# One transfer of X made four, and another order of the front, in an adaLN, H3 and SwiGLU kernel

## The chip, the cores and the metric

The kernel runs on one core of a Trainium2 chip. The metric is the device time of one execution in microseconds; the median of three runs before the change is 581.48 us (580.92 to 582.07).

## The reference, cut to what matters

One sequence of S = 2048 positions and D = 512 channels passes an adaLN layer with two branches. The first is the H3 operator: a causal convolution of 4 taps on K, a product with V, a causal convolution as long as the sequence, and a gate. The second is a SwiGLU feed-forward net with F = 1792.

```python
kv = shift_conv(k, shift_k) * v                  # 4 taps per channel
kv_f = rfft2(pad(kv)); kf_f = rfft2(pad(ssm_k))  # over 2 S points
y = irfft2(kv_f * kf_f)[:S] + kv * ssm_D
A = q * y                                        # q is layernorm(x)*(1+ca)+sa
...
mod = silu(c) @ w_mod                            # sa, ca, ga, sb, cb, gb
x = x + ga * A
h = layernorm(x) * (1 + cb) + sb
x = x + gb * ((silu(h @ w_gate) * (h @ w_up)) @ w_down)
```

Inputs and output are float32.

## The kernel before, in words

**Two parts.** The front (up to `next_psum()`) computes the H3 branch, the modulation rows, the second norm and the first two blocks of the feed-forward net. The main part is a loop over 28 steps (`gate_up_first`, `gate_up`) that does the rest of the feed-forward net with seven products of blocks for each eight; its first matmuls write the tiles named `a` and `b`.

**The front by chunks.** The 512 channels are four chunks `c_` of 128. For each chunk:

- `tap0`, `tap`, or `tms` with `tma`, make the short convolution, and `times_v` the product with V, in four pieces. Chunk 0 has its own way, by matmuls with diagonal tiles for one half (`diag`, `x0_taps`, `x0_mul`; tile `kvt`), and by VectorE for the other (`p_tap0`, `p_tap`, `p_mul`, turned by `p_turn`).
- `x_turn` brings the product to the layout of positions, `x_first` does the first stage of the transform (tile `s1`, in the profile `s`), `k_first` and `k_turn` the same for the kernel `ssm_k` (tiles `s` and `kt`). `skip` adds `ssm_D` to the first row of `ssm_k`.
- `swap_x(n)` transposes blocks of 32 by 32 of `X` in place on VectorE, a quarter of a chunk at a time.
- The second stage goes by half chunks `n`: `x3(n, m)` (tile `px`), `x_sum`, then `product3(n, m)` for m = 0, 1, 2 (a matmul into `pk`, and on VectorE the product with `xs`), and `inv3(n)`, 48 matmuls into `iv`, of which two copies on ScalarE write back to `X`.
- Chunk 0, 1 and 2 then need an exchange between partitions: `put(c_)` writes `X[c_]`, 128 partitions of 16 KB, to memory (`away`), and `get(c_)` reads it back in four transfers, one for each 32 partitions, transposed. Chunk 3 does it by VectorE (`inv3s`).
- `y_pe(t, chunks)` is the last stage of the transform (tile `y`), for the quarter `t` of the positions. `y_into` multiplies by the gate `s` and adds to `x`; `y_gate` and `add_y` do it in two steps.

The gate `s` is made from `x` by `do_stats` or `a_sum` and `a_var`, by `gate_n` (two rows of 512 each) and by `gate_p` (two operations with `bcs`). The modulation rows need `w_mod` in three parts of two halves, 1024 KB each (`mod_load(p, h)`, tile `wm`); parts 0 and 1 go over `mod_mul`, `mod_part` and `mod_bc`, part 2 over `mod_row(2, h)` (tile `mr`), `mod_out` and `mod_T`. Then `rs1` to `rs3`, `norm1`, `norm_t` (tile `nt`), `norm_s` and the splits into two parts (`hi1`, `lo1`) make the operands of the net, and `gu_pe` its first two blocks (tile `g`). `w8_hi` and `w8_lo` split the weights of those.

`warm(n)` is n matmuls of the identity with itself; nothing reads what they give.

**What sets the order.** Each engine does its instructions in the order of the program (`InOrder`). The front is one list of some 390 calls (from line 1204), in an order that is written out, and many calls name the engine (`e=act`, `e=dve`, `e=pool`). SyncE (SP) issues all DMAs of the front in the list's order; a `put` that waits for its data holds up the DMAs behind it. Which buffer a tile gets is written out too: `SLOTS` (line 53) has a string of digits for each pool, one digit for each allocation in the order of the list. The pool `ps` has four pairs of PSUM banks, so a matmul into a new tile waits until the tile that had this pair before has been read.

Of the kernel before, what the change touches and what calls it, by code (L numbers as in the profile page):

```python
# [43 lines left out]
def adaln_h3_swiglu(ctx, tc, q, k0, v0, kT, vT, ssm, dskip, wgu, wdn, wmod, e_fwd, e_inv, w_c, out):  # L44
# [9 lines left out]
        "e8": "301245670142561074612740340143104134104134104134150364051304650314056304",  # L54
        "b16": "0112345024024453024",
        "k2": "012021021020121020121020121020121020121020121012021012021012021012021012021012021012",
        "ps": "012301230123012031203120312031203120312013201320132013210321032103103210321032103210321032102310231023102310321032103210321213120023012120310",
        "r4": "01234012430012342013424301430123403402143201342014320134201432013420143240310234213014324031",
        "one": "456723017425036241736412506425173421750621507341573062570634170346250362417364125064251730256731546317027513643105725601341076526370140753623157047561321065745630120376546713025",
# [1143 lines left out]

    load_k0(0)
    diag(0, e=act)
    diag(2, e=dve)
    load_k0(1)
    warm(16)
    small_in(e=act)
    p_tap0(e=dve)  # L1210
    p_tap(1, 0, e=dve)
    p_tap(2, 0, e=dve)
    load_v0(0)
    load_k(1)
    silu_c()
    load_dskip()
    p_tap(1, 1, e=dve)
    p_tap(2, 1, e=dve)
    p_tap(3, 0, e=dve)
    diag(1, e=act)  # L1220
    diag(3, e=act)
    x0_taps(0)
    load_v0(1)
    x0_mul(0)
    tap0(1, e=act)
    load_e(0)
    load_e(1)
    p_tap(3, 1, e=dve)
    p_mul(1, e=pool)
    x0_taps(1)  # L1230
    p_mul(0, e=dve)
    p_turn(e=act)
    load_e(3)
    load_ssm(0, 0)
    load_e(2)
    x0_mul(1)
    x_first(0, 0, e=act)
# [12 lines left out]
    load_v(2)  # L1250
    swap_x(2)
    swap_x(3)
    k_first(0, 2, e=act)
    k_first(0, 1, e=act)
    times_v(1, 2, e=pool)
    k_first(0, 3, e=act)
    times_v(1, 1, e=pool)
    k_first(0, 0, e=act)
    tap0(2, e=act)
    warm(5)  # L1260
    k_turn(0, 0, e=act)
    k_turn(0, 1, e=dve)
    tap(2, 1)
    times_v(1, 0, e=pool)
    k_turn(0, 2, e=act)
    x_turn(1, 1, e=act)
    k_turn(0, 3, e=act)
    tap(2, 2)
    load_ssm(1)
    x_turn(1, 0, e=act)  # L1270
    k_first(1, 3, e=act)
    skip(1, e=pool)
    k_first(1, 0, e=act)
    x_first(1, 0, e=act)
    k_first(1, 1, e=act)
    k_first(1, 2, e=act)
    mod_rep(e=dve)
    x_first(1, 1, e=act)
    load_wc()
    load_k(3)  # L1280
    k_turn(1, 0, e=act)
    k_turn(1, 3, e=act)
    tap(2, 3)
    times_v(2, 0, e=pool)
    times_v(2, 1, e=pool)
    tap0(3, e=dve)
    x_turn(2, 0, e=act)
    times_v(2, 3, e=pool)
    x3(1, 1, e=act)
    swap_x(1)  # L1290
    load_x(1)
    x3(1, 2, e=act)
    swap_x(0)
# [23 lines left out]
    mod_mul(0, 0, e=act)
    load_ssm(2)
    product3(1, 2)
    product3(0, 1)  # L1320
    product3(0, 2)
    product3(1, 0)
    k_turn(1, 2, e=act)
    x_first(2, 1, e=act)
    swap_x(7)
    swap_x(5)
    load_v(3)
    mod_load(1)
    swap_x(8)
    mod_part(0, 0, e=pool)  # L1330
    load_x(0)
    tma(3, 3, 2, e=pool)
    load_einv()
    times_v(3, 1, e=pool)
    skip(2, e=dve)
    mod_mul(0, 1, e=act)
    times_v(3, 2, e=pool)
    inv3(1, e=act)
    inv3(0, e=act)
    put(0)  # L1340
    load_x(2)
    load_x(3)
    times_v(3, 3, e=pool)
    k_turn(1, 1, e=act)
    swap_x(10)
    x3(3, 2, e=dve)
    x3(2, 1, e=act)
    x3(3, 1, e=act)
    swap_x(9)
    skip(3, e=dve)  # L1350
    times_v(3, 0, e=pool)
    k_first(2, 0, e=act)
    k_first(2, 2, e=act)
    x_sum(3, e=dve)
    get(0)
    x3(2, 2, e=act)
    x_sum(2, e=pool)
    mod_mul(1, 0, e=act)
    mod_part(1, 0, e=pool)
    product3(3, 2)  # L1360
    product3(3, 0)
    product3(3, 1)
    mod_mul(1, 1, e=act)
    product3(2, 0)
    product3(2, 2)
    mod_part(1, 1, e=pool)
    mod_part(0, 1, e=pool)
    mod_part(0, 2, e=pool)
    do_stats(1, 0)
    mod_part(1, 2, e=pool)  # L1370
    product3(2, 1)
    k_first(2, 3, e=act)
    k_first(2, 1, e=act)
    x_turn(3, 0, e=act)
    inv3(3, e=act)
    inv3(2, e=act)
    do_stats(2, 0)
    k_turn(2, 0, e=act)
    x_turn(3, 1, e=act)
    k_turn(2, 1, e=act)  # L1380
    k_turn(2, 3, e=act)
    swap_x(11)
    put(1)
    get(1)
    x_first(3, 0, e=act)
    mod_part(0, 3, e=pool)
    mod_part(1, 3, e=pool)
    mod_bc(1)
    do_stats(0, 0)
    do_stats(0, 1)  # L1390
    do_stats(1, 1)
    x_first(3, 1, e=act)
    do_stats(2, 1)
    mod_bc(0)
    x3(5, 1, e=act)
    x3(5, 2, e=act)
    x3(4, 2, e=act)
    k_turn(2, 2, e=act)
    do_stats(3, 0)
    do_stats(3, 1)  # L1400
    x3(4, 1, e=act)
    x_sum(4, e=pool)
    swap_x(14)
    x_sum(5, e=pool)
    mod_mix()
    gate_n(2, 0, e=dve)
    k_first(3, 1, e=act)
    k_first(3, 0, e=act)
    k_first(3, 2, e=act)
    gate_n(0, 0, e=act)  # L1410
    gate_p(0, 0, 1, e=pool)
    load_w(1)
    k_first(3, 3, e=act)
    gate_n(3, 0, e=act)
    swap_x(15)
    swap_x(12)
    gate_n(0, 1, e=act)
    gate_p(0, 2, 1, e=pool)
    gate_n(1, 0, e=act)
    product3(4, 0)  # L1420
    product3(4, 2)
    gate_n(2, 1, e=act)
    product3(5, 0)
    product3(4, 1)
    product3(5, 1)
    product3(5, 2)
    swap_x(13)
# [18 lines left out]
    gate_p(3, 0, 1, e=dve)
    gate_p(3, 2, 1, e=pool)
    k_turn(3, 3, e=act)
    gate_p(0, 1, 1, e=dve)
    x3(6, 1, e=act)  # L1450
    y_into(0, 0, 1)
    x3(6, 2, e=act)
# [48 lines left out]
    y_gate(2, 2, 3)
    warm(5)
    norm_t(0, 1)
    norm_s(0, 1, e=act)
    acts_room()
    wd_hi(0)
    y_into(1, 0, 1)
    y_into(1, 2, 3)
    rs1(1)
# [4 lines left out]
    lo1("B11", 1, e=dve)
    norm_s(0, 3, e=act)
    lo1("B11", 0, e=pool)
    hi1("B21", 0, e=act)
    gate_p(3, 3, 1, e=pool)
    y_gate(3, 0, 1)
    add_y(3, 0, 4, (0, 1), e=dve)  # L1520
    rs2(1)
    rs3(1)
    y_pe(3, 2, 3)
    lo1("B21", 0, e=pool)
    y_gate(3, 2, 3)
    norm1(1, 0, e=act)
    norm1(1, 1, e=act)
    gu_pe(0, 0, 0)
    hi1("B21", 1, e=act)
    lo1("B21", 1, e=dve)  # L1530
    add_y(3, 0, 4, (2, 3), e=dve)
    norm1(1, 2, e=act)
    room()
# [245 lines left out]
```

## Time and profile before

| | before |
|---|---|
| median of the runs | 581.48 us |
| the profiled execution | 579.46 us |
| its span on the core | 577.7 us |
| granted TensorE clock | 1.00 |
| PE busy | 571.7 us (99%) |
| PE weight loads busy | 462.5 us (80%) |
| DVE busy | 448.3 us (78%) |
| ACT busy | 306.4 us (53%) |
| POOL busy | 318.0 us (55%) |

The difference between the profiled execution's time and its span, 1.8 us, lies around the span. PE is TensorE, PEld its weight loads, DVE is VectorE, ACT is ScalarE, POOL is GpSimd, SP is SyncE, whose queue (SPq) issues the DMAs. All operations are recorded at line 40, the helper that keeps the order, so the tiles' names tell them apart: `y<-X,ei` is the operation that reads `X` and `ei` and writes `y`.

A row of a timeline has start and length in us, the engine, the operation with its tiles, the number of records in it, and in brackets the recorded idle time before it and what ended it. Rows of PE carry the modelled end of the last matmul, so a row is a little longer than the distance to the next one. A row of the stretches has the window, its length and, for PE, PEld, DVE, ACT and POOL, the busy us with the number of instructions, then the granted clock, the DMA engines' share and GB/s. A row of groups has busy us and mean ns of one.

### The profile page before, as it was taken

The numbers are of one execution on the slowest core, as the hardware profiler recorded it, in microseconds if no ns is written. First come the engines' busy times: TensorE is split into PE (matmuls) and PEld (weight loads), VectorE is DVE, ScalarE is ACT, GpSimd is POOL, SyncE is SP. The second block draws the span as 40 slices with busy tenths as digits, with TensorE's granted clock in tenths as the row PEclk, the third lists the DMA queues.
The fourth block names the chain that finished last, engine by engine and source line by source line (L and its number), as shares of the span: only waits on it lengthen the run. The fifth ranks groups of instructions, "written<-read, shape, count | busy, mean of one in ns | idle before, by whom it ended". The sixth has DMA issues, their size and how long they took to land.

```text
span 577.7 us, 10729 instructions
## 1 busy us (share of the span) xinstructions
PE 571.7 (99%) x4262; PEld 462.5 (80%) x4262; DVE 448.3 (78%) x622; ACT 306.4 (53%) x471; POOL 318.0 (55%) x298
## 2 busy tenths in 40 slices
PE   9999999999999999999999999999999999999997
PEld 9985476546888888888887888888888888888886
DVE  4999999998998766666576579858686868686766
ACT  3999989951754544445454566343424343434330
POOL 1349897689737866757475676461606161515210
PEclk9999999999999999999999999999999999999999
DMA  8966998998215454284939970454343434343403
GB/s 315 411 256 261 379 251 227 235 235 205 69 37 200 148 216 165 40 281 145 283 140 257 250 319 1 149 190 171 117 160 124 160 123 161 127 162 127 163 1 145
DMA packets 54435, 106.98 MB, mean 185 GB/s; under 512 B 19441, under 2 KB 36209, under 8 KB 48370
## 3 DMA queue, kind: packets, MB, share of 16 engines
q1 hardware_dynamic: 54386, 106.31, 56.0%
q8 instruction: 33, 0.54, 0.4%
q14 instruction: 16, 0.13, 0.1%
HBM read 71.69 MB, written 34.60 MB: 184 GB/s over the span
## 4 chain that ended last, share of the span: by engine, by line
PE 86%; DVE 5%; DMA 4%; ACT 1%; SPq 1%; issue 1%; POOL 0%; ACTq 0%; POOLq 0%; DVEq 0%
PE a L40 22%; PE dn L40 14%; PE c L40 11%; PE b L40 6%; PE da L40 6%; PE s L40 4%; PE g L40 4%; PE dc L40 3%; PE iv L40 3%; PE pk L40 3%; DMA wm<-in_wmod 2%; PE kvt L40 2%; PE px L40 2%; DMA away<-X 1%; PE kt L40 1%; PE db L40 1%
## 5 line engine op out<-in xcount | busy, mean ns | idle before, releaser
L40 PE MATMUL a<-op,wsum 128*128 128x512 f32 x432 | 110.9, 392 | 0.3 <-ACT r L40 0.2
L40 PEld LDWEIGHTS a<-op,wsum 128*128 128x128 f32 x432 | 78.7, 188 | 15.7 <-ACT r L40 0.7
L40 PE MATMUL dn<-wd,acts 128*128 128x512 f32 x360 | 90.4, 389 | 0.0
L40 PEld LDWEIGHTS dn<-wd,acts 128*128 128x128 f32 x360 | 67.5, 188 | 14.0
L40 ACT COPY p<-a 128x512 f32<-128x512 f32 x50 | 29.3, 587 | 57.2 <-PE a L40 57.2
L40 POOL TENSOR_TENSOR wa<-ws,wa 128x512 fp32r<-128x512 f32 (+1 forms) x28 | 32.9, 1196 | 41.1 <-ACT wa L40 41.1
L40 DVE TENSOR_TENSOR x<-x,dn 128x512 f32<-128x512 f32 (+1 forms) x65 | 43.4, 672 | 12.8 <-PE dn L40 12.5
L40 POOL TENSOR_TENSOR tb<-wds 128x256 f32<-128x256 f32 x12 | 8.9, 740 | 64.1 <-DVE wds L40 64.1
L40 DVE TENSOR_TENSOR b<-r,c 128x512 f32<-128x512 f32 x24 | 16.7, 696 | 32.9 <-ACT sg L40 32.9
L40 ACT COPY r<-a 128x512 f32<-128x512 f32 x24 | 14.1, 586 | 50.7 <-PE a L40 50.7
L40 PE MATMUL c<-op,wa 128*128 128x512 f32 x156 | 40.0, 392 | 0.0
L40 PE MATMUL c<-op,wsum 128*128 128x512 f32 x156 | 39.6, 389 | 0.0
L40 DVE STREAM_TRANSPOSE X<-X 128x1024 f32<-128x1024 f32 x16 | 37.6, 2415 | 0.8 <-ACT X L40 0.8
L40 POOL TENSOR_TENSOR wsum<-sr,wsum 128x512 fp32r<-128x512 f32 x28 | 38.1, 1381 | 0.0
L40 PE MATMUL b<-op,wa 128*128 128x512 f32 x144 | 36.9, 391 | 0.0
L40 POOL TENSOR_TENSOR wd<-wds,wd 128x512 fp32r<-128x512 f32 x14 | 18.3, 1329 | 29.1 <-ACT wd L40 29.1
L40 PEld LDWEIGHTS c<-op,wsum 128*128 128x128 f32 x156 | 29.3, 188 | 6.1
L40 DVE TENSOR_TENSOR x<-x,da 128x512 f32<-128x512 f32 x48 | 32.7, 681 | 1.2 <-PE da L40 1.1
L40 PEld LDWEIGHTS c<-op,wa 128*128 128x128 f32 x156 | 28.5, 188 | 5.7 <-DVE b L40 0.4
L40 PEld LDWEIGHTS b<-op,wa 128*128 128x128 f32 x144 | 26.3, 188 | 4.9
L40 POOL TENSOR_TENSOR s<-s,bcs 128x512 f32<-128x512 f32 x22 | 28.0, 1287 | 0.9
L40 POOL TENSOR_TENSOR sr<-ws 128x256 f32<-128x256 f32 x28 | 24.8, 885 | 5.3 <-issue 4.4
(193 smaller groups left out, 1351.1 us busy)
## 6 DMA issues: line engine op xcount, KB each, us to landing
ds<-wsum SPq DMA_DIRECT2D x12, 1024.0 KB, 8.0
wsum<-ds SPq DMA_DIRECT2D x12, 1024.0 KB, 6.4
dw<-wa SPq DMA_DIRECT2D x12, 768.0 KB, 6.3
wa<-dw SPq DMA_DIRECT2D x12, 768.0 KB, 4.3
ws<-in_wgu SPq DMA_DIRECT2D x16, 512.0 KB, 5.4
wds<-in_wdn SPq DMA_DIRECT2D x14, 512.0 KB, 7.1
wm<-in_wmod SPq DMA_DIRECT2D x6, 1024.0 KB, 10.1
away<-X SPq DMA_DIRECT2D x3, 2048.0 KB, 11.8
```

What stands on the lines that cost most here:

```text
L40: return lambda *a, **k: self.tc.keep_in_program_order(f(*a, **k))
```

## The change: four transfers for one, and a new list

`put` is changed, all digit strings of `SLOTS` are new, and the list of the front is in another order, with another engine named in 35 of the calls; the diff is cut to the first lines of each. The calls are the same set, `warm` with 26 matmuls in all among them.

```diff
     def put(c_, name="away"):
         away[c_] = dp.tile([P, 32, P], F32, tag=f"{name}{c_}", name=f"{name}{c_}")
-        sp.dma_start(away[c_], X[c_])
+        for q_ in range(4):
+            sp.dma_start(away[c_][32 * q_ : 32 * q_ + 32], X[c_][32 * q_ : 32 * q_ + 32])
...
-        "b16": "0112345024024453024",
...
+        "b16": "0123450232053310453",
...
+    warm(5)
     load_k0(0)
+    load_k0(1)
     diag(0, e=act)
-    diag(2, e=dve)
-    load_k0(1)
     warm(16)
```

The `warm` calls stood at three places: 16 behind the first loads, 5 ahead of `k_turn(0, 0)`, 5 ahead of `norm_t(0, 1)`. Now 5 stand at the very start, 16 behind the first loads as before, and 5 ahead of `inv3(4)`. `x0_mul(1)` stood ahead of `tap(1, 1)` and now stands behind it. `w8_lo(1)` went from POOL to DVE and from behind `y_pe(0, 2)` to the place ahead of `y_into(0, 0, 1)`. Between `y_pe(0, 2)` and the first `norm_t` stood three calls of `y_pe`, and now stand four: `y_pe(3, 2, 3)`, `y_pe(2, 2, 3)`, `y_pe(1, 0, 1)`, `y_pe(1, 2, 3)`.

The calls that name another engine, by the engine they had and the one they have now:

| from, to | calls |
|---|---|
| ACT to DVE | diag(3), small_in, tap0(2), tms(3, 2), k_turn(1, 0), norm1(1, 1), hi1 of B21, second half |
| POOL to DVE | p_mul(1), x_sum(1), times_v(2, 0), tma(3, 2, 1), tma(3, 2, 2), mod_part(1, 1), gate_p(0, 2), gate_p(0, 3), gate_p(3, 2), w8_lo(1), lo1 of B21, first half |
| DVE to ACT | diag(2), k_turn(0, 1), mod_rep, tap0(3), x3(3, 2), gate_n(2, 0), norm_s(1, 3) |
| DVE to POOL | skip(0), skip(2), skip(3), times_v(2, 2), x_sum(3), gate_p(2, 2), gate_p(1, 0), gate_p(3, 0), lo1 of B11, second half, add_y(2, 0, 4, (0, 1)) |

Three places show what moved. The first is SP's queue around `put(2)`; `away_1498` and `X_558` before are chunk 2 with its copy in memory, `wm` is the third part of `w_mod`, `ws` and `wds` are weights of the net. Before:

```order
L40 DMA ws<-in_wgu 128x1024
L40 DMA away_1498<-X_558 128x4096
L40 DMA wm<-in_wmod 128x2048
L40 DMA X_558<-away_1498 32x32x128 x4
L40 DMA wm<-in_wmod 128x2048
L40 DMA ws<-in_wgu 128x1024 x2
L40 DMA wds<-in_wdn 128x2x512
```

After, with chunk 2 named `X_775` and `away_1511`, and the table of the last stage, `ei`, ahead of it:

```order
L40 DMA ei<-in_e_inv 128x2048
L40 DMA ws<-in_wgu 128x1024
L40 DMA away_1511<-X_775 32x4096 x4
L40 DMA wm<-in_wmod 128x2048 x2
L40 DMA X_775<-away_1511 32x32x128 x4
L40 DMA wds<-in_wdn 128x2x512
L40 DMA ws<-in_wgu 128x1024 x2
```

Four transfers of 32 partitions stand for one of 128, and both halves of `wm` are ahead of the four reads of `get(2)`, where one was.

The second place is the opening of DVE: `u` with `k` are the `p_tap` calls of chunk 0, `x` is `x0_mul`, `v` is `p_mul`, and `u` with `kt` and `sm` is `tap(1, t)`. Before:

```order
L40 TENSOR_SCALAR dg<-ident,k_96 128x128
L40 TENSOR_SCALAR u_120<-k_96 128x1024
L40 SCALAR_TENSOR_TENSOR u_120<-k_96,u_120 128x512 x5
L40 TENSOR_TENSOR x_153<-kvt,v_124 128x512
L40 SCALAR_TENSOR_TENSOR u_120<-k_96,u_120 128x512
L40 TENSOR_TENSOR v_124<-u_120,v_124 128x512
L40 TENSOR_TENSOR x_153<-kvt,v_124 128x512
L40 SCALAR_TENSOR_TENSOR u_155<-kt_126,sm,u_155 128x2047
```

After:

```order
L40 TENSOR_SCALAR u_124<-k_102 128x1024
L40 TENSOR_SCALAR dg<-ident,k_102 128x128
L40 COPY sm<-k_102 128x24
L40 SCALAR_TENSOR_TENSOR u_124<-k_102,u_124 128x512 x6
L40 TENSOR_TENSOR x_163<-kvt,v_126 128x512
L40 TENSOR_TENSOR v_126<-u_124,v_126 128x512 x2
L40 SCALAR_TENSOR_TENSOR u_168<-kt_132,sm,u_168 128x2047
L40 TENSOR_TENSOR x_163<-kvt,v_126 128x512
```

All six `p_tap` now stand ahead of the first product, both `p_mul` are on DVE, and the first tap of chunk 1 stands ahead of the second product with `kvt`.

The third place is ACT ahead of the copies that write chunk 2 back to `X` behind `inv3(4)` and `inv3(5)`. `s` with `x` and `rsa` are rows of `gate_n`, `kt` copies are those of `k_first(3, ...)`, and `bcs` with `pb` is `mod_bc(1)`. Before:

```order
L40 ACTIVATE s_1327<-x_718,rsa_1156 128x512 x2
L40 COPY kt_1293<-s_1334 128x4x4x32 x2
L40 ACTIVATE s_1290<-x_790,rsa_1265 128x512 x2
L40 ACTIVATE s_1327<-x_718,rsa_1156 128x512 x2
L40 ACTIVATE s_1353<-x_518,rsa_1167 128x512 x2
L40 ACTIVATE s_1290<-x_788,rsa_1198 128x512 x2
L40 COPY X_558<-iv 128x32x32 x4
```

After:

```order
L40 COPY kt_1285<-s_1321 128x4x4x32 x2
L40 COPY bcs<-pb_1343 128x2x512
L40 ACTIVATE s_1347<-x_877,rsa_1173 128x512 x2
L40 ACTIVATE s_1374<-x_773,rsa_1275 128x512 x2
L40 ACTIVATE s_1403<-x_729,rsa_1142 128x512 x2
L40 ACTIVATE s_1403<-x_888,rsa_1131 128x512 x4
L40 ACTIVATE s_1374<-x_773,rsa_1275 128x512 x2
L40 COPY X_775<-iv 128x32x32 x4
```

Twelve rows of `gate_n` and the copy of `mod_bc(1)` stand in a row between the last `kt` copies and the copies to `X`, where eight rows stood behind the last `kt` copies.

More of the change, by code (lines that the diff above doesn't have):

```diff
@@ L1219, in adaln_h3_swiglu @@
-    p_tap(3, 0, e=dve)
-    diag(1, e=act)
[L1221 to L1225, printed above, removed]
+    p_tap(3, 1, e=dve)
+    diag(2, e=act)
+    load_v0(1)
+    diag(1, e=act)
     load_e(0)
     load_e(1)
-    p_tap(3, 1, e=dve)
-    p_mul(1, e=pool)
+    p_tap(3, 0, e=dve)
+    load_ssm(0, 0)
+    x0_taps(0)
+    x0_mul(0)
+    p_mul(0, e=dve)
+    load_ssm(0, 2)
+    p_mul(1, e=dve)
+    tap0(1, e=act)
     x0_taps(1)
-    p_mul(0, e=dve)
+    load_e(2)
+    tap(1, 1)
@@ L1249, in adaln_h3_swiglu @@
+    skip(0, e=pool)
+    k_first(0, 0, e=act)
+    times_v(1, 0, e=pool)
+    swap_x(1)
+    load_ssm(1)
+    load_k(2)
+    times_v(1, 1, e=pool)
+    x_turn(1, 0, e=act)
+    skip(1, e=pool)
+    k_turn(0, 0, e=act)
+    k_turn(0, 3, e=act)
+    k_turn(0, 2, e=act)
+    load_wc()
+    k_turn(0, 1, e=act)
+    tap0(2, e=dve)
+    mod_load(1)
     times_v(1, 3, e=pool)
+    times_v(1, 2, e=pool)
+    x_turn(1, 1, e=act)
     load_v(2)
[L1251 to L1262, printed above, removed]
     tap(2, 1)
[L1264 to L1267, printed above, removed]
+    x3(1, 1, e=act)
     tap(2, 2)
-    load_ssm(1)
-    x_turn(1, 0, e=act)
+    x3(1, 2, e=act)
+    x_sum(1, e=dve)
     k_first(1, 3, e=act)
-    skip(1, e=pool)
+    k_first(1, 1, e=act)
     k_first(1, 0, e=act)
+    k_first(1, 2, e=act)
@@ L1274, in adaln_h3_swiglu @@
+    load_ssm(2)
+    load_k(3)
+    load_w(1)
     x_first(1, 0, e=act)
-    k_first(1, 1, e=act)
-    k_first(1, 2, e=act)
-    mod_rep(e=dve)
     x_first(1, 1, e=act)
[L1279 to L1282, printed above, removed]
+    mod_load(0)
     tap(2, 3)
[L1284 to L1293, printed above, removed]
+    times_v(2, 0, e=dve)
@@ L1317, in adaln_h3_swiglu @@
[L1317 to L1337, printed above, removed]
+    tms(3, 2, e=dve)
+    x_sum(0, e=pool)
+    product3(1, 0)
@@ L1338, in adaln_h3_swiglu @@
+    skip(2, e=pool)
+    product3(1, 1)
+    product3(1, 2)
+    k_turn(1, 0, e=dve)
+    mod_mul(1, 0, e=act)
+    times_v(2, 3, e=pool)
+    times_v(2, 2, e=pool)
+    tms(3, 3, e=act)
+    product3(0, 2)
+    product3(0, 1)
+    product3(0, 0)
+    swap_x(4)
+    mod_mul(1, 1, e=act)
+    tap0(3, e=act)
+    tap(3, 1)
     inv3(1, e=act)
     inv3(0, e=act)
-    put(0)
-    load_x(2)
-    load_x(3)
[L1343 to L1356, printed above, removed]
-    x_sum(2, e=pool)
[L1358 to L1363, printed above, removed]
+    load_v(3)
+    mod_part(1, 0, e=pool)
+    k_turn(1, 1, e=act)
+    load_ssm(3)
+    mod_part(1, 1, e=dve)
+    times_v(2, 1, e=pool)
+    x_turn(2, 0, e=act)
@@ new lines, in adaln_h3_swiglu @@
+    x_turn(2, 1, e=act)
+    tma(3, 2, 2, e=dve)
+    tma(3, 3, 2, e=pool)
+    tma(3, 2, 0, e=pool)
+    k_turn(1, 2, e=act)
+    load_x(2)
+    tma(3, 3, 0, e=pool)
+    k_turn(1, 3, e=act)
+    k_first(2, 0, e=act)
+    swap_x(5)
+    tma(3, 2, 1, e=dve)
+    put(0)
+    k_first(2, 3, e=act)
+    tma(3, 3, 1, e=pool)
+    load_x(0)
+    x_first(2, 0, e=act)
+    x_first(2, 1, e=act)
+    x3(2, 1, e=act)
+    mod_part(1, 2, e=pool)
+    swap_x(6)
+    x3(2, 2, e=act)
+    tma(3, 2, 3, e=pool)
@@ L1364, in adaln_h3_swiglu @@
+    tma(3, 3, 3, e=pool)
+    swap_x(7)
+    x3(3, 2, e=act)
+    x3(3, 1, e=act)
+    k_first(2, 2, e=act)
+    load_x(1)
+    do_stats(2, 0)
+    swap_x(11)
+    swap_x(10)
+    load_x(3)
+    k_first(2, 1, e=act)
+    x_sum(2, e=pool)
     product3(2, 0)
     product3(2, 2)
-    mod_part(1, 1, e=pool)
+    mod_mul(0, 0, e=act)
+    mod_rep(e=act)
+    product3(2, 1)
+    mod_mul(0, 1, e=act)
+    x_sum(3, e=pool)
+    product3(3, 0)
+    product3(3, 2)
+    mod_part(1, 3, e=pool)
+    product3(3, 1)
@@ L1367, in adaln_h3_swiglu @@
+    times_v(3, 1, e=pool)
+    inv3(2, e=act)
+    inv3(3, e=act)
+    times_v(3, 0, e=pool)
+    do_stats(0, 0)
+    x_turn(3, 0, e=act)
+    swap_x(9)
+    k_turn(2, 0, e=act)
+    mod_part(0, 0, e=pool)
+    k_turn(2, 1, e=act)
+    times_v(3, 3, e=pool)
+    times_v(3, 2, e=pool)
+    x_turn(3, 1, e=act)
+    k_turn(2, 2, e=act)
     mod_part(0, 1, e=pool)
     mod_part(0, 2, e=pool)
[L1369 to L1380, printed above, removed]
-    k_turn(2, 3, e=act)
[L1382 to L1397, printed above, removed]
@@ L1398, in adaln_h3_swiglu @@
-    k_turn(2, 2, e=act)
+    mod_part(0, 3, e=pool)
+    k_turn(2, 3, e=act)
     do_stats(3, 0)
     do_stats(3, 1)
+    do_stats(2, 1)
+    swap_x(8)
+    room()
+    x3(5, 1, e=act)
+    do_stats(1, 0)
+    do_stats(1, 1)
+    x_first(3, 0, e=act)
+    x_first(3, 1, e=act)
+    mod_bc(0)
+    x3(5, 2, e=act)
+    skip(3, e=pool)
+    x_sum(5, e=pool)
+    x3(4, 2, e=act)
+    get(0)
     x3(4, 1, e=act)
     x_sum(4, e=pool)
+    do_stats(0, 1)
+    put(1)
+    k_first(3, 1, e=act)
+    swap_x(15)
@@ L1403, in adaln_h3_swiglu @@
+    k_first(3, 0, e=act)
+    swap_x(12)
+    k_first(3, 2, e=act)
+    k_first(3, 3, e=act)
     swap_x(14)
-    x_sum(5, e=pool)
+    product3(5, 2)
+    mod_bc(1)
+    gate_n(1, 0, e=act)
     mod_mix()
[L1406 to L1409, printed above, removed]
+    product3(4, 1)
+    gate_p(1, 0, 1, e=pool)
+    product3(5, 1)
     gate_n(0, 0, e=act)
+    product3(4, 0)
+    get(1)
+    product3(4, 2)
     gate_p(0, 0, 1, e=pool)
-    load_w(1)
@@ L1413, in adaln_h3_swiglu @@
-    k_first(3, 3, e=act)
+    gate_n(2, 0, e=act)
     gate_n(3, 0, e=act)
-    swap_x(15)
-    swap_x(12)
+    gate_n(3, 1, e=act)
     gate_n(0, 1, e=act)
[L1418 to L1422, printed above, removed]
     product3(5, 0)
[L1424 to L1427, printed above, removed]
+    warm(5)
+    load_einv()
+    load_w(2)
     inv3(4, e=act)
@@ L1446, in adaln_h3_swiglu @@
[L1446 to L1452, printed above, removed]
+    gate_p(0, 2, 1, e=dve)
+    gate_p(0, 3, 1, e=dve)
+    gate_p(3, 0, 1, e=pool)
+    gate_p(3, 2, 1, e=dve)
+    gate_p(2, 0, 1, e=dve)
+    k_turn(3, 2, e=act)
+    k_turn(3, 1, e=act)
+    x3(6, 1, e=act)
+    x3(6, 2, e=act)
+    w8_lo(1, e=dve)
+    y_into(0, 0, 1)
+    x_sum(7, e=pool)
+    product3(7, 0)
+    product3(7, 1)
@@ L1500, in adaln_h3_swiglu @@
     hi1("B11", 0, e=act)
[L1501 to L1509, printed above, removed]
     norm_t(0, 2)
     norm_t(0, 3)
+    lo1("B11", 0, e=pool)
+    acts_room()
     norm_s(0, 2, e=act)
-    hi1("B11", 1, e=act)
[L1514 to L1533, printed above, removed]
+    norm_s(0, 3, e=act)
+    norm_t(0, 1)
+    add_y(2, 0, 4, (0, 1), e=pool)
+    y_pe(3, 0, 1)
+    y_gate(3, 0, 1)
+    gu_pe(0, 0, 0)
+    hi1("B21", 0, e=act)
+    hi1("B21", 1, e=dve)
+    norm_s(0, 1, e=act)
+    hi1("B11", 1, e=act)
@@ L1534, in adaln_h3_swiglu @@
+    lo1("B11", 1, e=pool)
     gu_pe(1, 0, 0)
```

193 lines of the change are left out of this document (92 added, 101 removed).

## The prediction

> **What bounds the kernel now.** I read the page first, then the chain of waits, then the stretches of 10 us, then each engine in order of time.
>
> ```profile
> span 577.7 us, 10729 instructions
> PE 571.7 (99%) x4262; PEld 462.5 (80%) x4262; DVE 448.3 (78%) x622; ACT 306.4 (53%) x471; POOL 318.0 (55%) x298
> PE 86%; DVE 5%; DMA 4%; ACT 1%; SPq 1%; issue 1%; POOL 0%; ACTq 0%; POOLq 0%; DVEq 0%
> ```
>
> The chain that ended last runs on PE for 86% of the span. Its pieces, in order of time, show where the front ends:
>
> ```profile
> 112.17 8.44 DMA away<-X
> ...
> 123.59 2.77 SPq L40
> ...
> 126.40 12.98 DMA wm<-in_wmod
> 139.43 1.09 PE mr L40 x16
> ...
> 182.11 1.36 PE a L40 x6
> 183.47 1.36 PE b L40 x6
> ```
>
> From 182.11 us PE works in groups of six matmuls that start every 1.36 us. The code behind that point is not edited, so 577.7 - 182.1 = 395.6 us are carried over, and the question is when the first `a` group starts. In the front, two stretches (busy us of PE, PEld, DVE, ACT, POOL, then clock and DMA share):
>
> ```profile
> 40.00:50.00 10.00, 10.00 (x166) 5.32 (x172) 10.00 (x7) 10.00 (x12) 6.53 (x6) 1.00 0.47 161
> ...
> 150.00:160.00 10.00, 10.00 (x73) 8.35 (x72) 9.80 (x22) 7.66 (x11) 6.29 (x6) 1.00 0.18 53
> ```
>
> PE and DVE are full together, and ACT is with them in the first. Which of them leads is seen on PE in order of time (start, us, tile, records, recorded idle before it):
>
> ```profile
> 1.35 5.61 PE L40 MATMUL warm<-ident 128*128 128x128 f32 x32 [1.35 <-POOL ident masks.py:199]
> 6.80 7.31 PE L40 MATMUL kvt<-dg,k 128*128 128x128 f32 x64
> ...
> 14.91 3.84 PE L40 MATMUL s<-x,er 64*128 64x128 f32 x64
> ...
> 22.25 1.38 PE L40 MATMUL warm<-ident 128*128 128x128 f32 x10
> 23.85 2.96 PE L40 MATMUL kt<-ident,kt 128*128 128x128 f32 x24 [0.22 <-ACT kt L40]
> ...
> 31.16 1.16 PE L40 MATMUL s<-er,ss 64*128 64x128 f32 x16 [0.23 <-POOL ss L40]
> ...
> 47.20 5.39 PE L40 MATMUL pk<-K,wc 64*32 64x512 f32 x96
> ...
> 55.59 5.41 PE L40 MATMUL iv<-xs,wc 32*64 32x512 f32 x96
> ...
> 99.45 5.38 PE L40 MATMUL pk<-K,wc 64*32 64x512 f32 x96
> 104.76 6.00 PE L40 MATMUL iv<-xs,wc 32*64 32x512 f32 x96
> ...
> 125.48 6.65 PE L40 MATMUL iv<-xs,wc 32*64 32x512 f32 x96
> ...
> 136.73 1.97 PE L40 MATMUL y<-X,ei 128*64 128x128 f32 x32
> 139.43 1.09 PE L40 MATMUL mr<-wm,crep 64*32 64x512 f32 x16 [0.74 <-DMA wm<-in_wmod]
> ...
> 147.87 0.66 PE L40 MATMUL nt<-ident,n 128*128 128x128 f32 x4
> 148.37 1.28 PE L40 MATMUL warm<-ident 128*128 128x128 f32 x10
> ```
>
> Equal work takes equal time: 96 records of pk last 5.39 and 5.38 us, 50 us apart. That is PE's own pace, and the recorded idle time in the whole front is 1.35 + 0.22 + 0.23 + 0.74 = 2.5 us. Two inverse stages are stretched over the 5.41 us of the first: by 0.6 us at 104.76 and by 1.2 us at 125.48. So **PE leads, with little to take away**: without its start, 1.2 us of waits and 1.8 us of stretch, 3.0 us of 579.46. The two fillers (`warm`, ten records each, which compute nothing needed) at 22.25 and 148.37 stand where PE would wait.
>
> [...]
>
> **The change part by part.** The calls of the front are the same set, with `warm` in all 26 times in both, so PE has no work less. What moves is who does a step, and when.
>
> *Who does it.* By the calls whose engine changes, VectorE gains `tms`, two pairs of `tma`-sized adds, `mod_part`, `w8_lo`, a `p_mul`, a `hi1` and a `norm1`, and gives away an `x3` copy, a `gate_n`, an `add_y`, three `skip` and a `norm_s`; the rest changes sides in pairs. Rows that price them:
>
> ```profile
> L40 DVE TENSOR_SCALAR u<-kt,sm 128x2048 f32<-128x2048 f32 x1 | 1.3, 1276 | 0.0
> L40 DVE COPY xs<-px 128x1024 f32<-128x1024 f32 x1 | 1.2, 1170 | 0.0
> L40 DVE TENSOR_TENSOR xs<-xs 128x512 f32<-128x512 f32 x2 | 1.3, 672 | 0.0
> L40 DVE TENSOR_TENSOR x<-x,s 128x1024 f32<-128x1024 f32 x4 | 5.3, 1336 | 0.0
> ```
>
> Gains: 1.3 + six adds of 0.67 + 0.7 + 0.7 + 0.6 = 7.3 us; losses: 1.2 + 1.0 + 1.3 + 0.9 + 0.8 = 5.2 us. So DVE has about 2 us more to do, and GpSimd some 6 us less. DVE's own waits hide it: 1.50 us at 14.14 and 0.76 us at 117.65 (rows below) are two of them. Added up row by row in the new order, DVE reaches the products of chunk 2 some 1 us before the time of this row:
>
> ```profile
> 100.72 3.48 DVE L40 TENSOR_TENSOR xs<-pk,xs 128x1024 f32<-128x1024 f32 x3
> ```
>
> Price 0; 2 us if that cover is gone.
>
> *The opening, to 38 us.* (a) `warm(5)` now stands ahead of `x0_taps`: ten records more, so kvt starts near 7.9 instead of 6.80: +1.1 (ten records at 22.25 took 1.1 to the next one's start, 1.38 with the last one's end). (b) No filler at 22.25 and no `tap0` on ACT ahead of `k_turn`: 23.85 - 22.25 = -1.6. (c) `x0_mul(1)` now stands behind `tap(1, 1)`.
>
> ```profile
> 7.13 3.65 DVE L40 SCALAR_TENSOR_TENSOR u<-k,u 128x512 f32<-128x512 f32 x5
> ...
> 14.14 0.69 DVE L40 TENSOR_TENSOR x<-kvt,v 128x512 f32<-128x512 f32 x1 [1.50 <-PE kvt L40]
> 14.75 4.73 DVE L40 SCALAR_TENSOR_TENSOR u<-kt,sm,u 128x2047 f32<-128x2047 f32 x2
> ```
>
> DVE comes to that tap near 13.6 (from 7.13 on six `p_tap` of 3.65 / 5 = 0.73 and three products of 0.69), needs 4.73 / 2 = 2.4 for it, and ends x0_mul(1) at 16.6; PE is done with `p_turn` at 7.9 + 7.15 + 0.97 = 16.0 (64 records of kvt without the last one's end, and eight more). +0.6. (d) `k_turn(0, 0)` waits for the last kt copies on ACT, whose row of copies starts 1.6 us later than now: between 0 and +0.5; I take +0.1, the end that is nearer to the row at 23.85, where PE waits 0.22. (e) `skip(1)` stands in a place where GpSimd has it done before PE asks: the 0.23 at 31.16 go. Sum (a) to (e): 0.0.
>
> *The middle, to 111 us.* The inverse of chunk 2 lies behind a filler and behind products in another order: its 0.6 us of stretch go. The filler costs 1.1, of which 0.7 lies in the wait for product3(4, 0): +0.4. Sum -0.2. ACT is late here:
>
> ```profile
> 102.25 5.96 ACT L40 ACTIVATE s<-x,rsa 128x512 f32<-128x512 f32 x8
> 107.91 2.11 ACT L40 COPY X<-iv 128x1024 f32<-128x1024 f32 x2
> ```
>
> Twelve `gate_n` rows of 5.96 / 8 = 0.745 us and the 1.1 us copy of `mod_bc(1)` stand ahead of the X<-iv copies, so these start near 110.0 instead of 107.91 and `put(2)` leaves near 113.8 instead of 112.17. PE, at 110.9 by then, finds its bank just free: 0 (below nothing no way leads, above it 1 us).
>
> *The end, to the first g group.* (f) `mod_load(2)` is issued ahead of `get(2)` and not behind it: the 0.74 us at 139.43 go. (g) `w8_lo(1)` (two adds, 1.4 us) is put ahead of `y_into(0, 0, 1)` on DVE, and `x3(6, 2)` takes that y's bank.
>
> ```profile
> 118.45 1.95 PE L40 MATMUL px<-X,wc 64*32 64x512 f32 x32
> ...
> 117.65 1.23 DVE L40 TENSOR_TENSOR y<-y,s 128x1024 f32<-128x1024 f32 x1 [0.76 <-ACT s L40]
> ```
>
> PE comes to x3(6, 2) near 119.7 (the px row holds both halves of `x3(6)`, so the second stands at 119.4 now; the 0.3 are what PE's rows in the new order add up to), and DVE ends that y at 117.65 + 1.23 + 1.4 = 120.3, or 120.6 if `s` is later by its 0.3: between 0 and +0.9, I take +0.5. (h) From the end of `y_pe(0, 2)` at 139.43 to norm_t(0, 0) at 147.87 are 8.4 us of DVE, GpSimd and ACT, unchanged. The new order has four `y_pe` of 1.85 in it (1.97 at 136.73, with the last one's end), 7.4 us, and no filler behind: -1.28 + 1.0 = -0.3.
>
> *The split of `put`.* The transfers' rows:
>
> ```profile
> X<-away SPq DMA_DIRECT2D x12, 512.0 KB, 10.9
> away<-X SPq DMA_DIRECT2D x3, 2048.0 KB, 11.8
> ```
>
> A `get` of one quarter needs one quarter's `put` only, so the first can leave up to 6 us (three quarters of 8.44) earlier; for chunks 0 and 1 the `get` stands a long way behind, and for chunk 2 its bytes queue behind mod_load's. I count 0. The chain row gives 22.3 us from put(2) to the last get(2)'s landing (123.59 issue plus 10.9); 113.8 + 22.3 = 136.1, and one more 1024 KB of wm ahead of it adds up to 3: 137 to 139, where `y_pe(0, 2)` asks near 139.0.
>
> Sum: 0.0 - 0.2 - 0.74 + 0.5 - 0.3 = **-0.7 us** on the profiled 579.46, whose span of 577.7 has 1.8 us around it. That execution lies 2.0 us under the median of the runs, 581.48, so the forecast is 580.7.
>
> **The rivals.** *More goes than I count.* The waits and stretches of 3.0 us go, (c), (d) and (g) cost nothing, because the new banks and order fit: 581.5 - 3.0 = 578.5. For it: DVE reaches chunk 2's products earlier by its rows. Against it: the stretch at 125.48 waits for DVE's products, and DVE gets no less work. *The last chunk comes late.* put(2) leaves 1.6 us later, and get(2) lands behind 139.0. From there every microsecond is paid, since the 8.4 us chain hangs on y_pe(0, 2) and PE has only 7.4 us to do beside it. If the four quarters do not overlap, each takes at least a part of the 6 to 11 us that a 512 KB transfer takes now; 4 us of lateness give 581.5 - 0.7 + 4 = 584.8. For it: slack of 0 to 2 us. Against it: the first get can leave early. [...]
>
> **How the numbers follow.** Forecast, level or a little ahead: 0.50, by itself 579.5 to 582.0. More goes: 0.25. Late chunk: 0.25. A measurement of this kernel tells 0.2%, 1.16 us, from no change. Of the forecast's half 0.17 lie past that on the fast side, 0.29 within, 0.04 on the slow side. So faster 0.42, same 0.29, slower 0.29. The range takes in both rivals' times: 578.2 to 584.8.
>
> **What would show it.** PE's kvt at 7.9; s<-x,er at 16.6; no recorded wait of mr; the filler of ten ahead of the iv of chunk 2; the wait ahead of x3(6, 2); the first `a` group at 181 to 182. I am wrong if PE's first `a` group moves by more than 2 us, or if the 395.6 us behind it change.

## The result: slower by 1.4%, with a wait for the last chunk

The changed kernel takes 588.51 us (four runs, 588.29 to 592.07), the one before 581.20 us in the same comparison. The ratio is 1.0139, with a 95% interval of 1.0115 to 1.0163. The profiled execution took 588.36 us, 1.8 us of it outside its span.

The page after has the same number of matmuls, and a clock that is no longer full:

```profile
span 586.6 us, 10729 instructions
PE 573.9 (98%) x4262; PEld 466.8 (80%) x4262; DVE 448.6 (76%) x624; ACT 305.7 (52%) x472; POOL 311.3 (53%) x295
PEclk9999999998899999999999999999999999999999
```

In the map of 40 slices the two slices from 132 to 161 us show 8 tenths of the clock. The chain of waits runs through the same place. Before, it went there through SP's queue and the load of `wm` to mr; now it goes through SP's queue and the last read of chunk 2 to `y`:

```profile
121.33 2.35 SPq L40
...
126.77 6.83 SPq L40
133.66 12.14 DMA X<-away
145.94 10.03 PE y L40 x144
...
189.64 1.36 PE a L40 x6
```

The first `a` group starts at 189.64 us and not at 182.11: 7.5 of the 8.9 us that the span is longer are lost in the front. Behind it 397.0 us are left, 395.6 before; 1.1 us of that is a wait for VectorE that was not there. PE in order of time has the whole loss in a few rows:

```profile
8.64 7.31 PE L40 MATMUL kvt<-dg,k 128*128 128x128 f32 x64
15.79 1.04 PE L40 MATMUL kvt<-ident,v 128*128 128x128 f32 x8
16.75 3.84 PE L40 MATMUL s<-x,er 64*128 64x128 f32 x64
...
121.23 1.09 PE L40 MATMUL px<-X,wc 64*32 64x512 f32 x16 [0.34 <-DVE x L40]
...
133.33 1.95 PE L40 MATMUL mr<-wm,crep 64*32 64x512 f32 x32
...
138.98 1.09 PE L40 MATMUL y<-X,ei 128*64 128x128 f32 x16
145.94 10.03 PE L40 MATMUL y<-X,ei 128*64 128x128 f32 x144 [5.87 <-DMA X<-away]
```

PE waits 5.87 us for the last read of chunk 2 ahead of `y_pe(0, 2)`. The y records behind it take 10.03 us; the same 144 take 8.08 us in experiment 1, so 1.95 us more go there. The stretches show why:

```profile
142.00:144.00 2.00, 0.00 (x0) 0.00 (x0) 0.45 (x3) 0.00 (x0) 1.92 (x3) 0.79 1.11 191
144.00:146.00 2.00, 0.06 (x2) 0.09 (x3) 0.00 (x0) 0.00 (x0) 0.97 (x1) 0.50 0.93 257
146.00:148.00 2.00, 2.00 (x20) 2.00 (x22) 0.05 (x1) 0.00 (x0) 0.00 (x0) 0.50 0.16 60
148.00:150.00 2.00, 2.00 (x22) 2.00 (x20) 1.93 (x5) 1.05 (x1) 0.00 (x0) 0.50 0.00 0
150.00:152.00 2.00, 2.00 (x42) 2.00 (x40) 1.97 (x9) 0.00 (x0) 0.91 (x1) 1.00 0.00 0
```

The clock falls to 0.50 while PE stands idle and stays there for 4 us of work: 20 and 22 records in 2 us, then 42. With the opening (kvt at 8.64 us, 6.80 before) the sum is 5.87 + 1.95 + 1.84 = 9.7 us; the mr wait of 0.74 and the filler of 1.28 us are gone from this place. That leaves 7.6, and all other moves cancel to 0.1.

SP's queue shows where the last read lost its time. Before, after, and with one put in the new order (experiment 1):

```profile
112.17 0.34 SPq L40 DMA_DIRECT2D away<-X  x1
118.56 0.33 SPq L40 DMA_DIRECT2D wm<-in_wmod  x1
120.62 5.73 SPq L40 DMA_DIRECT2D X<-away  x4
```

```profile
114.00 5.12 SPq L40 DMA_DIRECT2D away<-X  x4
119.90 3.78 SPq L40 DMA_DIRECT2D wm<-in_wmod  x2
123.79 12.59 SPq L40 DMA_DIRECT2D X<-away  x4
```

```profile
113.69 0.33 SPq L40 DMA_DIRECT2D away<-X  x1
119.47 0.80 SPq L40 DMA_DIRECT2D wm<-in_wmod  x2
121.94 9.52 SPq L40 DMA_DIRECT2D X<-away  x4
```

Each row has the start of the first issue and the time that the issues took together. Split, `put(2)` starts at nearly the same time as whole, yet the first read is issued 1.9 us later, not 6 us earlier, and the four reads are issued over 12.6 us, not 9.5. Their issue ends at 136.4 us; whole it ends at 131.5.

The packets point at the reason. The trace records every DMA packet with its start, length and size; a row of X is one packet of 16 KB. For the 128 packets of a `put` (with one to three strays), median length in us, and the sum over all in us of one DMA engine's time:

```
kernel                           put(0)       put(1)       put(2)
before                         0.61   82    0.61   85    0.61   82
after (4 of 32 neighbours)     0.61   96    0.71  111    1.28  157
1, one put                     0.61   81    0.61   83    0.62   81
3, before, 4 of 32 neighbours  0.61  101    0.81  116    1.28  158
5, 4 of 32, every fourth       0.61   80    0.61   85    0.62   81
7, 2 of 64 neighbours          0.61  103    1.25  137    1.28  152
9, 4 of 32, memory rows apart  0.61  102    0.77  116    1.28  158
10, 8 of 16, every eighth      0.61   94    0.97  126    1.22  148
```

Split by neighbours, the median packet of `put(2)` takes 1.28 us and not 0.61, though it moves the same 16 KB. Over 16 DMA engines, all at work, that is an estimate of 16 x 16384 B / 1.28 us = 205 GB/s against 430 GB/s.

### The profile page after: what moved, and what is told of

It is laid out like the page before. It is cut to its first block, busy times and chain, and to the rows that moved or that the text cites. A ratio compares the mean times of both kernels' runs of the same rounds, so it can differ in the third digit from the quotient of the medians.

```text
span 586.6 us, 10729 instructions
## 1 busy us (share of the span) xinstructions
PE 573.9 (98%) x4262; PEld 466.8 (80%) x4262; DVE 448.6 (76%) x624; ACT 305.7 (52%) x472; POOL 311.3 (53%) x295
## 4 chain that ended last, share of the span: by engine, by line
PE 85%; DMA 5%; ACT 4%; SPq 2%; DVE 2%; issue 1%; POOL 0%; ACTq 0%; POOLq 0%
PE a L40 21%; PE dn L40 12%; PE c L40 11%; PE da L40 6%; PE b L40 6%; PE g L40 4%; PE s L40 4%; PE iv L40 3%; PE dc L40 3%; PE pk L40 3%; PE kt L40 3%; PE px L40 2%; SPq L40 2%; PE y L40 2%; PE kvt L40 2%; DMA X<-away 2%
## 5 line engine op out<-in xcount | busy, mean ns | idle before, releaser
L40 POOL TENSOR_TENSOR wa<-ws,wa 128x512 fp32r<-128x512 f32 (+1 forms) x28 | 34.5, 1255 | 42.3 <-ACT wa L40 42.3
L40 DVE STREAM_TRANSPOSE X<-X 128x1024 f32<-128x1024 f32 x16 | 36.1, 2316 | 0.0
L40 POOL TENSOR_TENSOR xs<-xs 128x512 f32<-128x512 f32 x14 | 17.7, 1287 | 23.7 <-ACT xs L40 23.6
```

The costliest lines, as they stand in the source:

```text
L40: return lambda *a, **k: self.tc.keep_in_program_order(f(*a, **k))
```

## The experiments

My theories for the first four: A, the second half of `wm` ahead of `get(2)` delays it; B, the four transfers of `put(2)` are slow; C, `put(2)` only leaves later.

### 1. One put in the new order

```diff
-        for q_ in range(4):
-            sp.dma_start(away[c_][32 * q_ : 32 * q_ + 32], X[c_][32 * q_ : 32 * q_ + 32])
+        sp.dma_start(away[c_], X[c_])
```

> The changed kernel (588.5 us) with put as one transfer of 128 partitions again, the new order kept. Theory A (the second half of wm, 1024 KB, stands ahead of get(2) in the queue and its bytes make the last read of chunk 2 land late): the split does little, 587.5 to 589.5 us, and PE still waits 5 to 6.5 us for X<-away. Theory B (the four transfers of put(2) are what is slow): the wait goes and 581 to 583 us are left. Theory C (put(2) only starts later, and what was issued ahead of it is still under way): 587 to 589 us, as in A.

Measured: 580.00 us against 580.52 before, ratio 0.9999 (0.9984 to 1.0015). PE's wait in the timeline:

```profile
140.36 8.08 PE L40 MATMUL y<-X,ei 128*64 128x128 f32 x144 [0.94 <-DMA X<-away]
```

Theory B holds, and A and C fall as the main cause: with one transfer the new order is as fast as the old one, and the whole loss of some 8 us belongs to the split. The time is even below the 581 to 583 us that I gave to B.

### 2. The second half of wm behind get(2), put split

```diff
     mod_load(2, 0)
-    mod_load(2, 1)
...
     get(2)
+    mod_load(2, 1)
```

> The changed kernel with mod_load(2, 1) put behind get(2), where it stands in the kernel before; put stays split. Theory A: the last read lands 5 to 6 us earlier, the wait of 5.87 us for X<-away falls to under 1.5 us, the clock stays at 1.00, a wait of mr for wm of 0.5 to 2 us comes back: 581 to 583.5 us. Theory B and theory C: the wait shrinks by at most 2 us, 586 to 588.5 us.

Measured: 594.62 us, ratio 1.0250 (1.0226 to 1.0275); a miss for all three, worse than the change. The waits of PE:

```profile
PE mr L40 <- DMA wm<-in_wmod: 11.1, 1, 11.1
```

The wait moves from `X<-away` to `wm`. The last read of chunk 2 did land earlier, at 142.0 us and not at 145.8, but that is 3.8 us of the 5 to 6 that theory A gave, and the second half of `wm`, now behind the slow reads, is later still. The new order does both halves of `mod_row` early, so what stands behind the slow reads is late whichever it is.

### 3. The split in the old order

```diff
-        sp.dma_start(away[c_], X[c_])
+        for q_ in range(4):
+            sp.dma_start(away[c_][32 * q_ : 32 * q_ + 32], X[c_][32 * q_ : 32 * q_ + 32])
```

> The kernel before (581.2 us) with put split into four, its own order kept. Theory A: 580.5 to 582 us, the first reads of chunk 2 can leave earlier and nothing waits. Theory B: the last read of chunk 2 lands 4 us or more later and PE waits for it, 584 to 589 us. Theory C: as A.

The edit is made in the kernel before. Measured: 593.56 us, ratio 1.0201 (1.0142 to 1.0261). Theory B again, and more than it asked. PE's two waits:

```profile
106.33 5.37 PE L40 MATMUL pk<-K,wc 64*32 64x512 f32 x48 [3.63 <-DVE xs L40]
...
148.78 1.97 PE L40 MATMUL y<-X,ei 128*64 128x128 f32 x16 [4.98 <-issue]
```

The second stands at `y_pe(0, 2)`, as in the change; the profile names no cause, but the trace has the last read of chunk 2 landing at 148.6 us, just ahead of it. The first is VectorE's lateness, which begins with a load of x that stands behind `put(0)`:

```profile
80.87 0.70 DVE L40 BATCH_NORM_STATS2 bna<-x 128x6 f32<-128x512 f32 x1 [2.73 <-DMA x<-in_q]
```

So in this order the split of `put(0)` seems to cost too; no run splits it alone. The new order bears the split better than the old one (7.3 us against 13).

### 4. Both halves of wm ahead of get(2) in the old order, one put

```diff
     mod_load(2, 0)
+    mod_load(2, 1)
     get(2)
-    mod_load(2, 1)
```

> The kernel before with mod_load(2, 1) ahead of get(2), as the change has it; put stays one transfer. Theory A: the last read of chunk 2 lands 4 to 6 us later, PE waits 3 to 5 us for X<-away, its clock falls behind that for 4 us, the 0.74 us of mr go: 584 to 587 us. Theory B and C: the slack is enough, 580 to 581.5 us.

Measured: 583.16 us, ratio 1.0041 (1.0019 to 1.0063), between the theories:

```profile
140.70 1.09 PE L40 MATMUL y<-X,ei 128*64 128x128 f32 x16 [1.96 <-DVE x L40]
```

```profile
142.00:144.00 2.00, 2.00 (x22) 0.68 (x8) 1.93 (x6) 0.51 (x1) 1.81 (x2) 0.52 0.05 16
```

A further 1024 KB ahead of the reads does cost in that order: a wait of 1.96 us and a low clock behind it. The profile charges the wait to VectorE, but VectorE was done at 140.2 us; the last read of chunk 2 landed at 140.5 us, where it landed at 137.1 before, and `y` starts behind it.

### 5. Four transfers, each of every fourth partition

What in the split is slow? Theory P: the partitions that a transfer takes. Theory N: the number of transfers.

```diff
-            sp.dma_start(away[c_][32 * q_ : 32 * q_ + 32], X[c_][32 * q_ : 32 * q_ + 32])
+            sp.dma_start(away[c_][q_::4], X[c_][q_::4])
```

> The changed kernel with put still in four transfers of 32 partitions, but each takes every fourth partition (q, q + 4, q + 8, ...) instead of 32 neighbours. Theory P (32 neighbouring partitions are read by all DMA engines at half the rate: a packet of 16 KB of put(2) takes 1.28 us split and 0.61 us whole): packets of 0.61 to 0.7 us, no wait for X<-away over 1.5 us, 579.5 to 582 us. Theory N (it is the number of transfers and the two rows that each engine gets of one): as the changed kernel, packets of 1.2 to 1.3 us, 587 to 590 us.

Measured: 580.96 us, ratio 1.0003 (0.9982 to 1.0025), and packets of 0.62 us. Theory P: four transfers of 32 partitions cost nothing here when each is spread over all 128. In the profiled execution a short wait still came together with a low clock, and the 144 records of y took 10.99 us, not 8.08:

```profile
140.94 10.99 PE L40 MATMUL y<-X,ei 128*64 128x128 f32 x144 [0.97 <-DMA X<-away]
```

```profile
140.00:142.00 2.00, 1.06 (x10) 1.09 (x12) 1.92 (x5) 0.00 (x0) 1.92 (x2) 0.53 0.86 303
142.00:144.00 2.00, 2.00 (x24) 2.00 (x22) 1.35 (x4) 0.32 (x1) 1.92 (x3) 0.50 0.07 23
144.00:146.00 2.00, 2.00 (x22) 2.00 (x20) 1.93 (x11) 0.73 (x1) 0.90 (x1) 0.50 0.00 0
```

### 6. Four transfers of all partitions, a quarter of the columns each

```diff
-            sp.dma_start(away[c_][32 * q_ : 32 * q_ + 32], X[c_][32 * q_ : 32 * q_ + 32])
+            sp.dma_start(away[c_][:, 8 * q_ : 8 * q_ + 8], X[c_][:, 8 * q_ : 8 * q_ + 8])
```

> The changed kernel with put in four transfers of all 128 partitions and a quarter of the columns each (4 KB a row). Theory P: the bytes leave at the rate of one transfer, 579.5 to 582.5 us. Theory N: four issues as in the change, 585 to 590 us.

Measured: 581.46 us, ratio 1.0008 (0.9992 to 1.0025). Four transfers for one cost nothing that can be measured here; the packets, now of 4 KB, took 0.16 us in the median, about a quarter of 0.61. The wait is longer than in experiment 5, and the clock stayed at 1.00:

```profile
140.13 8.08 PE L40 MATMUL y<-X,ei 128*64 128x128 f32 x144 [1.63 <-DMA X<-away]
```

### 7. Two transfers of 64 neighbours

```diff
-        for q_ in range(4):
-            sp.dma_start(away[c_][32 * q_ : 32 * q_ + 32], X[c_][32 * q_ : 32 * q_ + 32])
+        for q_ in range(2):
+            sp.dma_start(away[c_][64 * q_ : 64 * q_ + 64], X[c_][64 * q_ : 64 * q_ + 64])
```

> The changed kernel with put in two transfers of 64 neighbouring partitions. Theory P: a packet of 16 KB takes between 0.61 and 0.8 us, the last read of chunk 2 lands at most 1.5 us later than with one transfer: 580 to 583 us. Theory N: half of the loss stays, 583 to 586 us.

Measured: 587.65 us, ratio 1.0119 (1.0089 to 1.0150), packets of 1.28 us and this wait:

```profile
146.75 10.34 PE L40 MATMUL y<-X,ei 128*64 128x128 f32 x144 [5.10 <-DMA X<-away]
```

A miss for both theories: 64 neighbours are as slow as 32. PE also waited 1.52 us for `wm` ahead of the second mr. So the rate did not grow with the count of neighbours from 32 to 64.

### 8. Only put(2) split

```diff
-        for q_ in range(4):
-            sp.dma_start(away[c_][32 * q_ : 32 * q_ + 32], X[c_][32 * q_ : 32 * q_ + 32])
+        n_ = 4 if c_ == 2 else 1
+        for q_ in range(n_):
+            r = slice(P // n_ * q_, P // n_ * q_ + P // n_)
+            sp.dma_start(away[c_][r], X[c_][r])
```

> The changed kernel with put(2) alone in four transfers of 32 partitions; put(0) and put(1) are one transfer each. Both theories: nearly all of the loss comes from put(2), whose packets are the slowest (157 engine-us after, 82 before, against 96 and 111 for the others) and which alone is waited for: 586 to 589 us, with 4.5 to 6 us of waiting for X<-away. If put(0) and put(1) cost too, by what they delay behind them: 583 to 586 us.

Measured: 588.34 us, ratio 1.0141 (1.0099 to 1.0183), with

```profile
145.60 9.78 PE L40 MATMUL y<-X,ei 128*64 128x128 f32 x144 [6.17 <-DMA X<-away]
```

In the new order `put(2)` alone carries the loss; `put(0)` and `put(1)` are covered.

### 9. The memory side spread, the partitions not

```diff
-            sp.dma_start(away[c_][32 * q_ : 32 * q_ + 32], X[c_][32 * q_ : 32 * q_ + 32])
+            sp.dma_start(away[c_][q_::4], X[c_][32 * q_ : 32 * q_ + 32])
...
-            m = away[c_][32 * q_ : 32 * q_ + 32].rearrange("p a d -> a p d")
+            m = away[c_][q_::4].rearrange("p a d -> a p d")
```

> The changed kernel, put in four transfers of 32 neighbouring partitions as in the change, but written to every fourth row of the copy in memory (and read back from there), so that only the memory side is spread. Theory S (the side of SBUF: neighbours in one half of the partitions are read at half the rate): packets of 16 KB stay at 1.2 to 1.3 us, 587 to 592 us. Theory M (the side of memory: 512 KB in one piece are written at half the rate): packets of 0.61 to 0.7 us, 579.5 to 582.5 us.

Measured: 588.19 us, ratio 1.0098 (1.0071 to 1.0125), packets of 1.28 us. Theory S: it is the side of SBUF, the memory on the core that holds `X`, and not the side of `away`.

### 10. Eight transfers, each of every eighth partition

```diff
-        for q_ in range(4):
-            sp.dma_start(away[c_][32 * q_ : 32 * q_ + 32], X[c_][32 * q_ : 32 * q_ + 32])
+        for q_ in range(8):
+            sp.dma_start(away[c_][q_::8], X[c_][q_::8])
```

> The changed kernel with put in eight transfers of 16 partitions, every eighth one, so that each transfer spans both halves. Theory H (it is only about a transfer lying in one half of the partitions): packets of 0.61 to 0.7 us, 580 to 583 us. [...] Theory N, number of transfers, would say more than the 588.5 us of the change.

Measured: 589.64 us, ratio 1.0144 (1.0123 to 1.0166), packets of 1.22 us. Theory H falls: spanning both halves is not enough. The time alone would fit theory N, which said more than 588.5 us; but N had fallen with four transfers in experiments 5 and 6. Every fourth partition gave packets of 0.62 us and every eighth 1.22; why, no run shows.

### 11. A filler in the wait

```diff
+    warm(22)
     y_pe(0, 2)
```

One digit is put into the string `ps` of `SLOTS` for the filler's bank.

> The changed kernel with a filler of 44 records of warm (4.7 us) ahead of y_pe(0, 2), where PE waits 5.87 us for the last read of chunk 2. If the low clock behind the wait (10.03 us for 144 records of y, 8.08 us in the run with one put) comes from PE standing idle: the clock stays at 1.00, the y records take 8.1 us, the time falls by 1.5 to 2.5 us, to 586 to 587 us. If it comes from something else, the time stays at 588 to 589 us.

Measured: 586.61 us, ratio 1.0083 (1.0065 to 1.0102), clock 1.000:

```profile
139.43 5.18 PE L40 MATMUL warm<-ident 128*128 128x128 f32 x44
145.74 8.08 PE L40 MATMUL y<-X,ei 128*64 128x128 f32 x144 [1.13 <-DMA X<-away]
```

```profile
146.00:148.00 2.00, 2.00 (x42) 2.00 (x40) 1.10 (x2) 0.00 (x0) 0.00 (x0) 1.00 0.14 56
```

The wait for the read is as long as ever, but PE is kept busy, and the y records take 8.08 us. The low clock came from the idle time, and cost 1.9 us.

### 12. One put, and the first filler moved into the wait

```diff
-    warm(5)
     load_k0(0)
...
+    warm(5)
     y_pe(0, 2)
```

The edit is made in the kernel of experiment 1, and the digit in `ps` moves with the call.

> The changed kernel with put in one transfer, and the five warm matmuls of the very start moved ahead of y_pe(0, 2). Kernel with one put alone: 580.0 us against 580.5 before, with a wait of 0.94 us there and runs from 579.3 to 583.4. Expected: the opening gives back 0.7 to 1.8 us, the filler fills the wait and the clock never falls there: 578 to 579.8 us, with no run over 581. If the order is at its limit elsewhere (DVE and ACT in the opening), 579.5 to 580.5 us.

Measured: 579.80 us (579.23 to 581.19) against 581.69 before, ratio 0.9971 (0.9961 to 0.9981): 1.7 us faster than the kernel before, and some 9 us faster than the change.

```profile
7.04 7.31 PE L40 MATMUL kvt<-dg,k 128*128 128x128 f32 x64
...
138.10 1.38 PE L40 MATMUL warm<-ident 128*128 128x128 f32 x10
139.58 8.08 PE L40 MATMUL y<-X,ei 128*64 128x128 f32 x144
```

The opening gives 1.16 us back (kvt at 8.20 in experiment 1), and no wait is recorded ahead of the y. One run of twelve was over 581 us, which I had not expected.

## Why the prediction was wrong, point by point

**The bound was read rightly.** PE led in the front, and the loss is PE's waiting, its low clock and its start. A move of more than 2 us in the first `a` group was named as what would prove me wrong, and it is 7.5.

**The order came out near its sum, in part by luck.** Forecast -0.7 us, measured 0.9999 for the order alone (experiment 1), which is 0 within 0.9 us and can't tell the forecast from no change. Of its terms:

- (a) kvt was forecast at 7.9, and 8.64 measured. The length of the same 42 records of warm lies between 6.37 and 7.63 us in ten profiles, 6.99 in the mean; that of 32 records is 5.84 in the mean of four. So +1.1 holds in the mean, and the +1.84 here is what two single executions drew.
- (c) s<-x,er was forecast at 16.6 and stands at 16.75, by luck. It starts 8.11 us behind kvt, as before, and `x0_mul(1)` on DVE ends only at 17.16 us. So PE didn't wait for that product, as I had thought, and the +0.6 of (c) cost nothing; the late kvt hid it.
- (f) The mr wait is gone. (g) The wait ahead of x3(6, 2) was taken as 0.5 and is 0.34.

**The step that failed is the split of `put`**: "A `get` of one quarter needs one quarter's `put` only, so the first can leave up to 6 us (three quarters of 8.44) earlier ... I count 0". It took for granted that four quarters move at the rate of the whole. They move at 205 GB/s and not at 430, so `put(2)` holds the DMA engines for 157 / 16 = 9.8 us and not 81 / 16 = 5.1. The last issue of the reads ends 4.9 us later than with one put, and the wait is 5.87 - 0.94 = 4.9 us longer: the whole difference arrives at PE, and the idle time adds 1.95 us of low clock, for which the sum had no term. For the last landing of chunk 2 the prediction gave 137 to 139 us; it came at 140.1 us with one put and at 145.8 us split. The part that is missing even with one put fits the 10.9 us of that sum, which is the median of twelve reads: before, the last read of chunk 2 landed 13.5 us after its issue, 2.6 us more.

**The rival "the last chunk comes late" had the place right and the size wrong.** It gave 584.8 us, by 4 us of lateness out of queueing, which was my estimate, and no term for the clock; the runs show 4.9 us and 1.95 us. Four transfers for one cost nothing that can be measured in experiments 5 and 6 (580.96 and 581.46 us).

**What I should have weighed.** No row that I quoted has a transfer that leaves from a part of the partitions, so the price of 0 for the split was an estimate without a measurement under it. The runs give the missing rates, estimated from the packets of 16 KB over 16 DMA engines as above: 205 GB/s for 32 and for 64 neighbours (1.28 us), 430 GB/s for all 128 (0.61 us), 423 GB/s for every fourth partition (0.62 us) and 215 GB/s for every eighth (1.22 us). In these runs the rate went with the partitions that a transfer takes: experiment 5 had the full rate with 32 that lie four apart, the change half of it with 32 neighbours. What in the hardware makes the difference was not shown.

**What stays open.** Why `put(0)` and `put(1)` slow down less when split (medians of 0.61 and 0.71 us) was not tried. Other transfers beside them are not the reason: after, 66 of the packets of `put(0)` took under 0.7 us with no packet of another size under way at their middle. The trace doesn't record a packet's partitions.

## What to carry to other kernels

Where a transfer is split to let its parts be read earlier, look at the partitions of each part. Here a split in four cost nothing when each part still spread over all partitions, by columns or by every fourth partition (581.46 and 580.96 us in experiments 6 and 5, against 581.02 before). In `put(2)`, halves and quarters of neighbours ran at half the rate, two transfers as four (1.28 us for a packet of 16 KB, against 0.61 for the whole). In a queue that serves several streams, price a slower transfer by what stands behind it in that queue, and add the clock that a waiting PE loses: here 4.9 us and 1.95 us. Where a wait of PE can't be removed, matmuls that nothing needs, put into it, kept the clock at 1.00 here (experiments 11 and 12).

## What had not been expected of the hardware

- The low clock comes in steps. The trace records each change of the granted clock. It stood at 0.50 for 6.83 us after (143.16 to 149.99 us) and in experiments 3 (twice), 5, 7, 8 and 9, for 3.41 us in experiment 4, 10.24 us in experiment 10 and 13.65 us in experiment 2: one, two, three or four times 3.41 us. The full clock ahead of it had lasted 136.53 us after, 40 times 3.41. In these traces, then, the clock changes on a grid of 3.41 us.
- The length of a wait alone didn't decide. In experiment 5 the clock fell at 140.11 us, 0.14 us into the wait of 0.97 us, so the wait alone doesn't explain the fall; the 16 matmuls of one column each (pm, 1.95 us) stand close ahead of it. In the profiled execution of experiment 6 a wait of 1.63 us was followed by no fall, yet five of its ten executions had a mean clock of 0.997 and took 581.5 to 582.5 us, where the others took 580.0 to 581.4. What counts as idle was not tried, and what decides between the two is not shown.
- PE's first matmuls are slow for a time that changes between executions of the same program text: 42 records of warm took 6.46 us in experiment 11 and 7.46 us after, with the opening unchanged, where 44 records in the wait of experiment 11 took 5.18 us. The trace has the clock rise to full at 4.53 us in the one and at 6.63 us in the other, and in all ten profiles with 42 records a later rise goes with a longer warm (from 6.37 us at 4.34 to 7.63 us at 6.99).
